# Half of the first x tile through a transposing DMA instead of TensorE

## The chip, the cores and the metric

The kernel runs on one core of a Trainium2 chip. The metric is device time of one execution in microseconds (us), median of several runs. In the profile PE is TensorE's matmuls, PEld its weight loads, DVE VectorE, ACT ScalarE, POOL GpSimd, and SP the engine that here only issues DMAs; `SPq` is its queue of instructions.

## The reference

x is 2048 x 512 in bf16. Two branches read it and a gate per row mixes them.

```python
x = A_x
g = _sigmoid((x * gate_w).sum(-1, keepdims=True))
a = _A_ref(x, A_wq, A_wk, A_wv, A_wo, A_beta)   # attention in 4 segments of 512 rows, 32 heads of 16, with a running memory
b = _B_ref(x, B_W_gate, B_W_up, B_W_down)       # ReLU-gated MLP, 512 -> 1792 -> 512
return g * a + (1 - g) * b
```

Every projection contracts over x's columns, and the kernel feeds each segment to TensorE transposed (`xT`, columns on the partitions); its gate also reads the segment in natural layout (`xn`).

## The kernel before

The kernel is written as a graph of operations. A list scheduler with fixed guessed durations puts them in one order and picks buffers; then the instructions are emitted in that order. Segments 1 to 3 of x come by transposing DMA. Segment 0 is in a hurry: it comes in natural layout, in four quarters over the two DMA queues (SP and ACT), TensorE transposes it in 16 blocks into PSUM (`G`), and DVE and ACT copy the result to `xT`. The q projection of segment 0 runs step by step over the four blocks of 128 columns, so it can begin with half of x.

```python
for i in range(2):                    # halves of x's columns
    for eng, q, h in (("SP", nc.sync, 0), ("ACT", nc.scalar, 1)):
        ...  q.dma_start(out=xn[0].t[:, 2*h:2*h+2, 256*i:256*i+256], in_=x[...])
    if i == 0:   ...                  # wq block 0: one half of its columns on SP, one on ACT
    else:        ...                  # wq block 1 on SP, blocks 2 and 3 on ACT
...                                   # cut: then wk, wv, gate_w and the MLP weights on SP
def first_x(c, after):                # block c of 128 columns
    for h in range(2):
        ...  nc.tensor.transpose(gv[:, t*P:(t+1)*P], xn[0].t[:, 2*h+t, c*P:(c+1)*P], ident[:])
        ...  # DVE copies h == 0 to xT, ACT copies h == 1
first_x(0, None); first_x(1, None)
for ci in range(NC):                  # the four q steps, 4 matmuls each
    ...  nc.tensor.matmul(qS.t[:, c, :], lhsT=wq_sb[:, ci, ...], rhs=xT[0].t[:, ci, :], ...)
    if ci < 2:
        first_x(ci + 2, o_q0)
...                                   # cut: k projection, v projection, attention units, MLP
order = sc.run()
for o in order:
    tiling[0] = o.ran                 # "C": a dense matmul next to column-tiled work
    o.emit(o.eng)                     #      is emitted as four column tiles
```

Emitted as column tiles, a dense matmul takes 4 weight loads and 4 matmuls instead of one each.

Of the kernel before, what the change touches and what calls it, by code (L numbers as in the profile page):

```python
# [9 lines left out]
ACT = mybir.ActivationFunctionType  # L10
ALU = mybir.AluOpType

P = 128
# [5 lines left out]
L = S // NSEG  # L19
F = 1792  # L20
NC = D // P
# [33 lines left out]
class Sched:  # L55
# [5 lines left out]
    def op(self, name, engs, emit, deps=(), key=0.0, cls=1, mode=None, alloc=(), uses=(), land=0.0, flex=False):  # L61
        o = Op()
        o.flex, o.ran = flex, mode
        o.name, o.engs, o.emit, o.key, o.cls, o.mode = name, engs, emit, key, cls, mode
        o.alloc, o.uses = list(alloc), list(alloc) + list(uses)
        o.deps = [d if isinstance(d, tuple) else (d, None) for d in deps]
        o.deps = [d for d in o.deps if d[0] is not None]
        o.start = o.end = o.eng = None
        o.land = land
        o.succ, o.seq = [], len(self.ops)  # L70
        for b in o.uses:
            b.left += 1
        self.ops.append(o)
        return o
# [92 lines left out]
def kernel(  # L167
# [15 lines left out]
    nc = tc.nc  # L183
    x = A_x.flatten_outer_dims()
# [5 lines left out]
    def tl(name, shape, dt=BF16):  # L190
        return sb.tile(list(shape), dt, name=name)
# [9 lines left out]
    wq_sb, wk_sb, wv_sb, wo_sb = (tl(n, [P, NC, D]) for n in ("wq_sb", "wk_sb", "wv_sb", "wo_sb"))  # L201
# [98 lines left out]
    def load(name, emit, nbytes, key, alloc=(), uses=(), deps=(), eng="SP"):  # L300
        o = op(name, {eng: 0.5}, emit, deps=[(d, None) for d in deps] + ([(last_dma[0], -1e9)] if eng == "SP" else []),
               key=key, cls=0, alloc=alloc, uses=uses, land=nbytes / GBs)
        if eng == "SP":
            last_dma[0] = o
        return o

    xn = [Buf(xnp) for _ in range(NSEG)]
    xT = [Buf(xTp) for _ in range(NSEG)]

    def wview(ap):  # L310
        return ap.rearrange("(c p) n -> p c n", p=P)

    lx0, lw, lwq = {}, {}, {}
    for i in range(2):
        for eng, q, h in (("SP", nc.sync, 0), ("ACT", nc.scalar, 1)):
            def f(e, i=i, q=q, h=h):
                q.dma_start(out=xn[0].t[:, 2 * h:2 * h + 2, 256 * i:256 * i + 256],  # L317
                            in_=x[256 * h:256 * h + 256, 256 * i:256 * i + 256].rearrange("(t p) d -> p t d", p=P))
            lx0[i, h] = load(f"x0_{i}{h}", f, 131072, -300 + i, eng=eng, alloc=[xn[0]] if (i, h) == (0, 0) else [],
                             uses=[] if (i, h) == (0, 0) else [xn[0]])  # L320
        if i == 0:
            for eng, q, h in (("SP", nc.sync, 0), ("ACT", nc.scalar, 1)):
                def f(e, h=h, q=q):
                    cs = slice(256 * h, 256 * h + 256)
                    q.dma_start(out=wq_sb[:, 0, cs], in_=A_wq[0:P, cs])  # L325
                lwq.setdefault(0, []).append(load(f"wq0{h}", f, 65536, -299.5, eng=eng))
        else:
            for c0, c1, eng, q in ((1, 2, "SP", nc.sync), (2, 4, "ACT", nc.scalar)):
                def f(e, c0=c0, c1=c1, q=q):
                    q.dma_start(out=wq_sb[:, c0:c1, :], in_=A_wq[c0 * P:c1 * P, :].rearrange("(c p) n -> p c n", p=P))  # L330
                o = load(f"wq{c0}", f, 131072 * (c1 - c0), -298, eng=eng)
                for ci in range(c0, c1):
                    lwq[ci] = [o]

    def loadw(name, tile_, ap, c0, c1, key, eng="SP"):
        def f(e):
            q = nc.sync if eng == "SP" else nc.scalar
            q.dma_start(out=tile_[:, :, c0:c1], in_=wview(ap)[:, :, c0:c1])
        return load(name, f, P * tile_.shape[1] * (c1 - c0) * 2, key, eng=eng)

    lw["wk"] = loadw("wk", wk_sb, A_wk, 0, D, 1)
    lw["wv"] = loadw("wv", wv_sb, A_wv, 0, D, 1)

    def f(e):
        nc.sync.dma_start(out=gwrep[:], in_=gate_w.partition_broadcast(P))
# [36 lines left out]
    xc0 = {c: [] for c in range(NC)}  # L382
    def first_x(c, after):
        for h in range(2):
            g = Buf(G)

            def f(e, c=c, g=g, h=h):
                gv = g.t[:].bitcast(BF16)
                for t in range(2):
                    nc.tensor.transpose(gv[:, t * P:(t + 1) * P], xn[0].t[:, 2 * h + t, c * P:(c + 1) * P], ident[:])  # L390
            a = op(f"xtr{c}{h}", {"PE": 0.2}, f, deps=[lx0[c // 2, h], o_ident, (after, 0.0)], key=-500 + c, mode="D",
                   alloc=[g], uses=[xn[0]])

            def f(e, c=c, g=g, h=h):
                gv = g.t[:].bitcast(BF16)[:, 0:256]
                dst = xT[0].t[:, c, 256 * h:256 * h + 256]
                if e == "DVE":
                    nc.vector.tensor_copy(dst, gv)
                else:
                    nc.scalar.activation(dst, gv, ACT.Copy)  # L400
            xc0[c].append(op(f"xcp{c}{h}", {"DVE": 0.27} if h == 0 else {"ACT": 0.4}, f, deps=[a], key=-500 + c, cls=0,
                             alloc=[xT[0]] if (c, h) == (0, 0) else [], uses=[g] + ([] if (c, h) == (0, 0) else [xT[0]])))
    qS = Buf(Spool)
    q0 = [Buf(QTp) for _ in range(NC)]
    o_q0 = None
    first_x(0, None)
    first_x(1, None)
    for ci in range(NC):
        def f(e, ci=ci):
            for c in range(NC):  # L410
                nc.tensor.matmul(qS.t[:, c, :], lhsT=wq_sb[:, ci, c * P:(c + 1) * P], rhs=xT[0].t[:, ci, :],  # L411
                                 start=(ci == 0), stop=(ci == NC - 1))
        o_q0 = op(f"q0.{ci}", {"PE": 4 * MM * (1.5 if ci < 2 else 1)}, f,
                  deps=xc0[ci] + lwq[ci] + [(o_q0, 0.0) if ci else None],
                  key=-400 + ci, mode="D", alloc=[qS] + q0 if ci == 0 else [], uses=([] if ci == 0 else [qS]) + [xT[0]])
        if ci < 2:
            first_x(ci + 2, o_q0)
    xc0 = [o for c in range(NC) for o in xc0[c]]
    xr = {0: xc0}
    for s in range(1, NSEG):  # L420
        if s > 1:
# [606 lines left out]
```

## Time and profile before

| | before |
|---|---|
| time, median of 3 (lowest, highest) | 267.25 us (266.84, 267.45) |
| profiled span | 265.7 us |
| PE busy | 256.3 us, 96% |
| first matmul of the k projection | 9.78 us |
| start of the last matmul | 262.15 us |

The last two rows are read from PE's timeline; the last matmul is the fourth of the second line:

```profile
9.78 0.59 PE L249 MATMUL G<-xT,wk_sb 128*128 128x512 bf16 x2
261.82 0.60 PE L249 MATMUL G<-wo_sb,oT 128*128 128x256 bf16 x4
```

The execution that was profiled took 267.44 us, at the slow end of the kernel's runs. Before 9.78 us is the *opening*, in which PE waits for loads; after it comes the *later part*, 252.37 us from the first k matmul to the last matmul, in which PE has work nearly all the time.

### The profile page before, as it was taken

What the parts mean: (1) busy time and instruction counts of PE and PEld (TensorE: products, weight loads), DVE (VectorE), ACT (ScalarE), POOL (GpSimd) and SP (SyncE); (2) the same over time, 40 slices, a digit from 0 to 9 for tenths busy, and PEclk for the clock granted to TensorE, in tenths of its full rate; (3) what the DMA queues carried; (4) which work ended last, traced back from release to release, by engine and by line L of the source; (5) the groups of instructions that cost most, each with busy time, mean ns of one, the idle gap of its engine ahead of it and who ended that gap; (6) DMA issues with size and microseconds to landing.
All of it is one profiled execution on the core that took longest, in us unless ns stands there. A gap on an engine that the chain in (4) does not pass through costs nothing.

```text
span 265.7 us, 7041 instructions
## 1 busy us (share of the span) xinstructions
PE 256.3 (96%) x2795; PEld 114.5 (43%) x2832; DVE 182.5 (69%) x404; ACT 195.3 (73%) x191; POOL 188.4 (71%) x467
## 2 busy tenths in 40 slices
PE   7999999999999999999999999999999999999995
PEld 6434444444444444444444434344443444444444
DVE  1397888888975185998888837688985725466611
ACT  3498999899886658899896667898788566777010
POOL 8268888888559688798648988887878866537000
PEclk9999999999999999999999999999999999999999
DMA  6995991016310000000660010000000010000011
GB/s 171 309 268 145 333 241 25 2 38 78 103 23 23 22 20 22 0 2 0 131 109 3 23 42 21 2 0 2 0 2 4 0 42 20 23 2 0 2 41 39
DMA packets 27585, 15.54 MB, mean 58 GB/s; under 512 B 13600, under 2 KB 27552, under 8 KB 27552
## 3 DMA queue, kind: packets, MB, share of 16 engines
q1 hardware_dynamic: 26592, 14.50, 23.2%
q10 hardware_dynamic: 960, 0.59, 0.7%
q8 instruction: 22, 0.36, 0.6%
q14 instruction: 11, 0.09, 0.1%
HBM read 9.84 MB, written 2.10 MB: 45 GB/s over the span
## 4 chain that ended last, share of the span: by engine, by line
PE 95%; issue 2%; DMA 2%; SPq 0%; DVE 0%; DVEq 0%
PE G L249 74%; PE S L740 9%; PE G L852 7%; PE G L247 2%; DMA wq_sb<-in_A_wq_dram 2%; PE S L411 1%; PE G L613 1%; PE G L787 0%; SPq L317 0%; DVE os L702 0%; SPq L325 0%; PE G L390 0%; DVEq L702 0%
## 5 line engine op out<-in xcount | busy, mean ns | idle before, releaser
L754 ACT ACTIVATE E<-S 128x2048 bf16<-128x2048 f32 x72 | 135.1, 1876 | 32.1 <-PE S L740 29.4
L762 POOL TENSOR_SCALAR_AFFINE_SELECT E<-E 64x256 bf16<-64x256 bf16 x256 | 116.2, 454 | 39.2 <-ACT E L754 25.4
L249 PE MATMUL G<-xT,wu_sb 128*128 128x512 bf16 x210 | 57.1, 380 | 0.4 <-issue 0.2
L249 PE MATMUL G<-xT,wg_sb 128*128 128x512 bf16 x207 | 56.3, 380 | 1.1 <-issue 0.8
L665 DVE TENSOR_TENSOR hT<-G,rg 128x512 bf16<-128x512 f32 x56 | 38.2, 683 | 20.0 <-ACT rg L661 10.9
L249 PE MATMUL G<-wd_sb,hT 128*128 128x512 bf16 (+1 forms) x215 | 49.7, 366 | 1.3 <-issue 1.1
L887 DVE STREAM_TRANSPOSE T<-G 128x512 f32<-128x512 f32 x44 | 30.3, 702 | 13.0 <-PE G L852 8.2
L661 ACT ACTIVATE rg<-G 128x512 bf16<-128x512 f32 x56 | 32.7, 597 | 5.6 <-PE G L249 5.3
L249 PEld LDWEIGHTS <-wu_sb 128*128 128x128 bf16 x218 | 19.9, 98 | 24.8 <-issue 3.0
L249 PEld LDWEIGHTS <-hT 128*128 128x128 bf16 x226 | 20.5, 98 | 22.7 <-issue 3.0
L249 PEld LDWEIGHTS <-wg_sb 128*128 128x128 bf16 x218 | 19.4, 98 | 24.6 <-issue 4.1
L740 PE MATMUL S<-QT,K 32*128 32x192 bf16 (+7 forms) x512 | 28.6, 287 | 0.5
L740 PEld LDWEIGHTS <-K 32*128 32x128 bf16 x512 | 8.3, 92 | 30.2 <-issue 29.7
L702 DVE TENSOR_SCALAR os<-G,ngcol 128x512 bf16<-128x512 f32 (+1 forms) x8 | 5.5, 683 | 21.1 <-PE G L249 21.0
L852 PE MATMUL G<-E,Vp 64*32 64x128 bf16 (+7 forms) x512 | 19.0, 284 | 0.4 <-issue 0.4
L852 PE MATMUL G<-E,VS 64*32 64x128 bf16 (+7 forms) x512 | 18.4, 284 | 0.0
L599 POOL COPY VS<-Vp 64x256 bf16<-64x256 bf16 x32 | 12.9, 404 | 7.5 <-DVE Vp L517 6.0
L704 ACT ACTIVATE os<-G,ngcol 128x512 bf16<-128x512 f32 x9 | 6.2, 687 | 15.9 <-PE G L249 15.8
L249 PE MATMUL G<-wo_sb,oT 128*128 128x512 bf16 (+1 forms) x66 | 17.0, 367 | 0.3 <-issue 0.3
L907 DVE TENSOR_TENSOR O<-T,sm 128x256 bf16<-128x256 f32 x32 | 16.0, 529 | 0.3
L249 PE MATMUL G<-xT,wk_sb 128*128 128x512 bf16 x60 | 15.8, 380 | 0.3 <-issue 0.2
L481 POOL COPY R<-rcol 32x4 f32<-32x4 f32 x64 | 13.6, 212 | 3.0
(96 smaller groups left out, 295.5 us busy)
## 6 DMA issues: line engine op xcount, KB each, us to landing
out_dram<-os SPq DMA_DIRECT2D x15, 128.0 KB, 1.7
wd_sb<-in_B_W_down_dram SPq DMA_DIRECT2D x1, 1792.0 KB, 13.9
xn<-in_A_x_dram SPq DMA_DIRECT2D x3, 512.0 KB, 4.9
wg_sb<-in_B_W_gate_dram SPq DMA_DIRECT2D x2, 512.0 KB, 5.3
wu_sb<-in_B_W_up_dram SPq DMA_DIRECT2D x2, 512.0 KB, 6.6
wg_sb<-in_B_W_gate_dram SPq DMA_DIRECT2D x3, 256.0 KB, 6.7
wu_sb<-in_B_W_up_dram SPq DMA_DIRECT2D x3, 256.0 KB, 6.4
wk_sb<-in_A_wk_dram SPq DMA_DIRECT2D x1, 512.0 KB, 5.9
```

What stands on the lines that cost most here:

```text
L249: nc.tensor.matmul(out_ap, lhsT=lhsT, rhs=rhs, start=start, stop=stop)
L481: nc.gpsimd.tensor_copy(R[s][32 * j:32 * j + 32, k, :], rcol[32 * k:32 * k + 32, cols])
L599: nc.gpsimd.tensor_copy(VS[s].t[64 * r:64 * r + 64, t, 0:H // 2 * HP].rearrange("p (h v) -> p h v", v=HP)[:, :, 0:DH], src[:, :, r, 0:DH])
L661: nc.scalar.activation(rg.t[:], g.t[:], ACT.Relu)
L665: nc.vector.tensor_tensor(h.t[:], u.t[:], rg.t[:], ALU.mult)
L704: nc.scalar.activation(ob.t[:, cs], g.t[:, 0:W], ACT.Copy, scale=ngcol[:, tt:tt + 1])
L740: nc.tensor.matmul(sp.t[:, j, off:off + w], lhsT=K2[s, cc].t[rows, kb, :, :].rearrange("p r k -> p (r k)"), rhs=QT[s, cc].t[rows, L - w:L] ...
L754: nc.scalar.activation(eb_.t[:], sp.t[:], ACT.Exp, scale=SCALE)
L762: nc.gpsimd.affine_select(out=v, in_=v, compare_op=ALU.is_ge, fill=0.0, base=0, pattern=[[0, 4], [1, 64]], channel_multiplier=-1)
L852: nc.tensor.matmul(gs[r].t[32 * j:32 * j + 32, L - w:L], lhsT=v, rhs=src.t[rows, j, off:off + w], start=(kb == 0), stop=(kb == 7), tile_po ...
L887: nc.vector.transpose(T.t[:].rearrange("p b e -> p (b e)"), g.t[:])
L907: nc.vector.tensor_tensor(O.t[:, :, r, :], T.t[:, :, 0:DH], sm.t[:, r, :, None].to_broadcast([P, 16, DH]), ALU.mult)
```

## The change

The intent: take half of the transposes and copies off the engines in the opening. The second half of x's columns goes by transposing DMA straight to `xT`; its natural copy, which only the gate needs, comes after wv. The loads of wq are redistributed.

```diff
-    for i in range(2):
-        ... x halves on SP and ACT; wq block 0 split over both; block 1 on SP; blocks 2, 3 on ACT
+    x0_part(0, 0, "SP", -300)
+    x0_part(0, 1, "ACT", -300)
+    wq_rows(0, 1, "ACT", -299)
+    def f(e):
+        nc.sync.dma_start_transpose(out=xT[0].t[:, 2:4, :], in_=x[0:L, 256:512])
+    lxt0 = load("xT0", f, 2 * 262144, -299, alloc=[xT[0]])
+    wq_rows(1, 2, "ACT", -298)
+    wq_rows(2, 4, "SP", -298)
     ... wk, wv
+    for h in range(2):
+        x0_part(1, h, "SP", 1)
 ... (cut)
     first_x(1, None)
+    xc0[2] = xc0[3] = [lxt0]
     for ci in range(NC):
         ...
-        if ci < 2:
-            first_x(ci + 2, o_q0)
```

Because the graph changes, the list scheduler also puts the *rest* of the program in another order. The diff doesn't show that.

More of the change, by code (lines that the diff above doesn't have):

```diff
@@ L313 @@
     lx0, lw, lwq = {}, {}, {}
-    for i in range(2):
-        for eng, q, h in (("SP", nc.sync, 0), ("ACT", nc.scalar, 1)):
-            def f(e, i=i, q=q, h=h):
-                q.dma_start(out=xn[0].t[:, 2 * h:2 * h + 2, 256 * i:256 * i + 256],
-                            in_=x[256 * h:256 * h + 256, 256 * i:256 * i + 256].rearrange("(t p) d -> p t d", p=P))
-            lx0[i, h] = load(f"x0_{i}{h}", f, 131072, -300 + i, eng=eng, alloc=[xn[0]] if (i, h) == (0, 0) else [],
-                             uses=[] if (i, h) == (0, 0) else [xn[0]])
-        if i == 0:
-            for eng, q, h in (("SP", nc.sync, 0), ("ACT", nc.scalar, 1)):
-                def f(e, h=h, q=q):
-                    cs = slice(256 * h, 256 * h + 256)
-                    q.dma_start(out=wq_sb[:, 0, cs], in_=A_wq[0:P, cs])
-                lwq.setdefault(0, []).append(load(f"wq0{h}", f, 65536, -299.5, eng=eng))
-        else:
-            for c0, c1, eng, q in ((1, 2, "SP", nc.sync), (2, 4, "ACT", nc.scalar)):
-                def f(e, c0=c0, c1=c1, q=q):
-                    q.dma_start(out=wq_sb[:, c0:c1, :], in_=A_wq[c0 * P:c1 * P, :].rearrange("(c p) n -> p c n", p=P))
-                o = load(f"wq{c0}", f, 131072 * (c1 - c0), -298, eng=eng)
-                for ci in range(c0, c1):
-                    lwq[ci] = [o]
@@ new lines, in x0_part, with wq_rows, f @@
+    def x0_part(i, h, eng, key):
+        def f(e):
+            (nc.sync if eng == "SP" else nc.scalar).dma_start(
+                out=xn[0].t[:, 2 * h:2 * h + 2, 256 * i:256 * i + 256],
+                in_=x[256 * h:256 * h + 256, 256 * i:256 * i + 256].rearrange("(t p) d -> p t d", p=P))
+        first = not lx0
+        lx0[i, h] = load(f"x0_{i}{h}", f, 131072, key, eng=eng, alloc=[xn[0]] if first else [], uses=[] if first else [xn[0]])
+    def wq_rows(c0, c1, eng, key):
+        def f(e):
+            (nc.sync if eng == "SP" else nc.scalar).dma_start(
+                out=wq_sb[:, c0:c1, :], in_=A_wq[c0 * P:c1 * P, :].rearrange("(c p) n -> p c n", p=P))
+        o = load(f"wq{c0}", f, 131072 * (c1 - c0), key, eng=eng)
+        for ci in range(c0, c1):
+            lwq[ci] = [o]
@@ L335, in loadw, with f @@
+    x0_part(0, 0, "SP", -300)
+    x0_part(0, 1, "ACT", -300)
+    wq_rows(0, 1, "ACT", -299)
+    def f(e):
+        nc.sync.dma_start_transpose(out=xT[0].t[:, 2:4, :], in_=x[0:L, 256:512])
+    lxt0 = load("xT0", f, 2 * 262144, -299, alloc=[xT[0]])
+    lxt0.engs["SP"] = 1.2
+    wq_rows(1, 2, "ACT", -298)
+    wq_rows(2, 4, "SP", -298)
     def loadw(name, tile_, ap, c0, c1, key, eng="SP"):
@@ L401, in first_x @@
             xc0[c].append(op(f"xcp{c}{h}", {"DVE": 0.27} if h == 0 else {"ACT": 0.4}, f, deps=[a], key=-500 + c, cls=0,
-                             alloc=[xT[0]] if (c, h) == (0, 0) else [], uses=[g] + ([] if (c, h) == (0, 0) else [xT[0]])))
+                             uses=[g, xT[0]]))
     qS = Buf(Spool)
@@ L415 @@
                   key=-400 + ci, mode="D", alloc=[qS] + q0 if ci == 0 else [], uses=([] if ci == 0 else [qS]) + [xT[0]])
-        if ci < 2:
-            first_x(ci + 2, o_q0)
-    xc0 = [o for c in range(NC) for o in xc0[c]]
+    xc0 = xc0[0] + xc0[1] + [lxt0]
     xr = {0: xc0}
```

## The prediction

> **What bounds the kernel now.** I read the busy shares first, then the chain that ended last, then that chain in order of time over the first 15 us, then PE's own timeline there, and last the sync engine's timeline, because the change touches only the opening.
>
> ```profile
> span 265.7 us, 7041 instructions
> PE 256.3 (96%) x2795; PEld 114.5 (43%) x2832; DVE 182.5 (69%) x404; ACT 195.3 (73%) x191; POOL 188.4 (71%) x467
> PE 95%; issue 2%; DMA 2%; SPq 0%; DVE 0%; DVEq 0%
> ```
> PE is busy 96% of the span and makes up 95% of the chain; no other engine passes 73%. The stretches (width, then busy time by engine, granted clock, DMA share, GB/s) tell where PE's idle 9.4 us are:
>
> ```profile
> 0.00:4.00 4.00, 2.89 (x28) 2.90 (x29) 0.47 (x11) 1.15 (x1) 3.33 (x8) 1.00 0.44 108
> 4.00:10.00 6.00, 5.18 (x36) 2.63 (x36) 1.10 (x4) 1.78 (x7) 4.60 (x8) 1.00 0.95 290
> 10.00:262.00 252.00, 247.76 (x2734) 108.89 (x2769) 180.50 (x388) 192.36 (x185) 180.52 (x452) 1.00 0.23 53
> 262.00:265.70 3.70, 0.42 (x4) 0.13 (x2) 0.48 (x1) 0.00 (x0) 0.00 (x0) 1.00 0.09 25
> ```
> From 10 us to 262 us PE is 98.3% busy at full clock. So a microsecond saved before 10 us moves the whole rest forward one for one, and nothing that eases DVE, ACT or POOL can pay. The opening is different: there the chain in order of time holds a DMA.
>
> ```profile
> 2.27 4.63 DMA wq_sb<-in_A_wq_dram
> 6.96 1.04 PE S L411 x4
> 7.99 0.22 PE G L390 x4
> 8.22 0.22 PE S L411
> 8.43 0.05 issue
> 8.48 1.46 PE S L411 x6
> 9.94 3.88 PE G L249 x18
> ```
> The load of the second row block of wq, issued at 2.27, ends PE's wait at 6.90. L411 is the first q projection, four steps of four matmuls; L390 is a TensorE transpose of x. The k projection (L249) follows. PE's timeline (start, length) between:
>
> ```profile
> 4.07 0.62 PE L390 MATMUL G<-ident,xn 128*128 128x128 bf16 x8
> 4.93 1.02 PE L411 MATMUL S<-xT,wq_sb 128*128 128x512 bf16 x4 [0.25 <-DVE xT L398]
> 6.34 0.48 PE L390 MATMUL G<-ident,xn 128*128 128x128 bf16 x4 [0.39 <-DMA xn<-in_A_x_dram]
> 6.96 1.04 PE L411 MATMUL S<-xT,wq_sb 128*128 128x512 bf16 x4
> ```
> The second half of x (columns 256 to 511) holds PE until 6.34, just before wq does. Both arrive late because the queues issue four loads each, about 0.5 us apart, and the first byte moves only at about 2.2 us.
>
> [...] the later 512 KB transposes of x land in 4.1 to 5.7 us (one in traffic 9.0), a plain 512 KB load of x in 4.9; but the rate seen while one runs is nearer 200 to 290 GB/s. [...] with both queues filled, 4 to 10 us moved 290 GB/s, and from 10 to 16 us, with SP alone, about as much or a little more. [...] Here one shows 219 ns, and eight took 0.62 us from first start to last end, so they overlap and cost about 0.1 us each. [...] The trace shows a small price: a row-tiled score group between dense groups starts 0.96 us after the dense group's start instead of 0.87 (22.38 to 23.34), and the next dense group 0.33 us later (23.67).
>
> **The change part by part.**
>
> Removed from PE: 8 of 16 transposes. Four took 0.22 us on the chain; the other four stood in 6.34 to 6.96, in the shadow of the wq load that came at 6.90. So 0.2 us is certain, up to 0.8 if data no longer waits. Also gone: two DVE copies (0.29 each) and two ACT copies (0.38 each)[...]; with PE as the bound they count only through PE's wait for the second half.
>
> Moved: x's second half becomes one SP transposing DMA in second place; wq's block 0 goes whole to ACT (second place), block 1 to ACT (third), blocks 2 and 3 to SP, behind the transpose. SP and ACT then issue eight loads without a wait, and these include wk and wv; before, wk waited on a landing and was issued at 3.78.
>
> When does each thing land? The issue times and landing times are from these rows and from the page of DMAs:
>
> ```profile
> 1.31 0.44 SPq L325 DMA_DIRECT2D wq_sb<-in_A_wq_dram  x1
> 3.78 0.38 SPq L338 DMA_DIRECT2D wk_sb<-in_A_wk_dram  x1
> 12.30 5.41 SPq L360 DMA_TRANSPOSE xT<-in_A_x_dram  x1
> ```
> - First half of x: as before, PE transposes at 4.07; first q step at 4.93 (wq block 0, 128 KB issued near 1.3, should land by 4.6: it took 2.9 us for 64 KB, and 64 KB more is 0.2 us at 290 GB/s, plus sharing with the transpose).
> - wq block 1: issued near 1.8 instead of 2.27; at 3.4 to 4.6 us in flight it lands between 5.2 and 6.4. Second q step from about 5.9, end 6.8 (four matmuls, 0.22 us apart, are 0.87).
> - Transposed half: issued near 1.3. A quiet 512 KB transpose holds SP for 1.3 to 2.0 us, one of 128 KB for 1.2, the one behind a full queue 5.41. I take 1.3 us for 256 KB here, when the queue is still short. Landing: 4 us after issue, near 5.5; not needed before 6.8.
> - wq blocks 2 and 3: issued near 2.7, and the same load took 5.0 us before: 7.3 to 7.7. Steps three and four then run 7.4 to about 9.2.
> - wk: issued near 3.2, took 5.9: near 9.1, as the steps end. Before, the k projection began at 9.78.
> Sum: the k projection begins near 9.2 instead of 9.78 to 9.94, a gain of 0.6 to 0.7 us. A check by bytes: x, wq and wk are 1.5 MB in both kernels, some 5.4 us at 290 GB/s; from 2.2 that allows 7.6[...]. So bytes don't forbid 9.2[...].
>
> Added: natural x columns 256 to 511 are still loaded (256 KB), after wv. That is extra traffic of 256 KB, 0.9 us at 290 GB/s, ahead of the gate weights. Those were issued at 6.51 and took up to 6.7, 13.2, while the first gate matmul ran at 16.33: 3 us of slack, hidden. The gating sums that read this copy run at 18.7 us and later, hidden too.
>
> Changed order: the list scheduler reorders the rest of the program. I counted the built programs: the same matmuls but for the eight transposes (and four dense ones no longer split into column tiles), and 172 changes of tiling mode against 170. A score group costs 0.33 + 0.09 = 0.42 us over the dense rhythm, of which 0.22 is its own stream of 512 columns: about 0.1 us per change, so 0.2 us lost.
>
> Net: 0.65 gained, 0.2 given back, about 0.45 us: 267.25 - 0.45 = **266.8 us**.
>
> **The rivals.**
> A, **the transpose blocks the queue**: if it holds SP 2.7 us (half of 5.41), wq blocks 2 and 3 are issued near 4.0, land near 9, and q ends near 10.8, wk behind it near 10.5. That costs 0.9 us: 268.3. For it: the 5.41 us row. Against: that one followed 1 MB of queued weights; quiet ones took 1.3 and 2.0.
> B, **hidden anyway**: wk's arrival binds, as the trace's 0.24 us wait of the weight load on wk before 9.69 suggests, and the bytes come no sooner. Then the k projection starts near 9.7 and the time stays at 267.2 to 267.4.
> C, **the order decides**: some later stage meets a score group or a value product that isn't ready. The kernel before idles 4.24 us between 10 and 262; a fifth more or less of that is 0.8 us either way.
> D, **everything early**: if all loads come by 7.3, the k projection starts at 8.6, gain 1.3 minus 0.2: 266.1.
>
> **Range and chances.** D and a lucky order give about 265.6, A with a little of C 268.3. The runs of before spread from 266.84 to 267.45. So 265.6 to 268.3 for 8 in 10. Two per cent are 5.3 us, more than half of PE's whole idle time: faster 0.01. Slower by 5.3 would need a stall that nothing in the trace shows: 0.02. Same: 0.97.
>
> **What would show it.** Right: L390's counterpart has 8 matmuls; the first k matmul starts between 8.6 and 9.5; wk issued near 3.2; the transpose is busy on SP for about 1.3 us; PE's idle from 10 us on stays within 1 us of 4.24. Wrong: SP stuck in the transpose past 3.5 us or the first q step later than 5.2 (rival A), a wait of PE for wk with a start near 9.7 (B), or an equal gain at 10 us that has vanished by the end (C). A total over 269 would mean that a wait for gate weights or for the score chain arose that I put down as hidden.

Beside two figures belongs what the trace of before shows. The flight of 3.4 to 4.6 us for wq block 1 was the estimate: that block took 4.6 us, and the four x loads of the same 128 KB took 2.7 to 4.7. The "first byte at about 2.2 us": from 1.8 to 2.1 us 38 GB/s moved, from 2.1 to 2.4 us 114, from 2.4 to 2.7 us 273.

## More of the kernel before

All runs quoted here were fast, with a granted TensorE clock of 0.998 to 1.000.

PE's own instructions come through a DMA queue too, and one line of the page that I passed over at first becomes important:

```profile
q8 instruction: 22, 0.36, 0.6%
```

That is 22 transfers of 16 KB over the execution (number, MB, share of 16 engines). That the queue is PE's is read from counts: no other engine has more than 531 instructions in these traces, and in the three kernels below that have 156 to 180 PE instructions fewer, it carries 21 transfers.

## The result and the profile after

| | before | changed |
|---|---|---|
| time, median of 4 (lowest, highest) | 267.16 us (266.84, 267.45) | 267.63 us (267.31, 267.82) |
| ratio, 95% interval | | 1.0017 (0.9999 to 1.0034) |
| profiled span | 265.7 us | 265.9 us |
| first k matmul | 9.78 us | 9.59 us |
| later part (first k matmul to last matmul) | 252.37 us | 252.78 us |

A ratio here is the mean time of one kernel's fast runs over that of the other's from the same rounds, so it isn't quite the ratio of the medians. Two more measurements of the same two kernels gave 1.0020 (0.9999 to 1.0041) and 1.0034 (1.0018 to 1.0051): slower by some 0.2 to 0.3%, 0.5 to 0.9 us in the medians.

The page and the stretches of the changed kernel (stretch, width, busy time of PE, PEld, DVE, ACT, POOL, clock, DMA share, GB/s) first:

```profile
span 265.9 us, 7000 instructions
PE 256.3 (96%) x2776; PEld 114.2 (43%) x2812; DVE 184.3 (69%) x404; ACT 192.8 (73%) x187; POOL 188.3 (71%) x467
```
```profile
4.00:10.00 6.00, 4.68 (x27) 2.04 (x26) 0.52 (x2) 0.87 (x3) 4.61 (x8) 1.00 1.11 283
10.00:262.00 252.00, 248.08 (x2720) 108.89 (x2754) 182.87 (x390) 190.49 (x183) 180.37 (x452) 1.00 0.21 53
```

The shares are those of before. From 4 to 10 us PE did 0.5 us less work, as it should with 8 transposes fewer, in the same six microseconds: the relief was mostly turned into waiting. The busy time from 10 to 262 us is even higher than before, although that part turns out longer; matmul ends are modelled and some records are missing, so this figure can't resolve half a microsecond. The page of before has 2,795 matmuls for 2,832 weight loads, that of the changed kernel 2,776 for 2,812. Run 2 below has a matmul for every weight load, and PE's idle time there is 0.85 us, not 4:

```profile
10.00:262.00 252.00, 251.15 (x2768) 108.38 (x2766) 180.69 (x389) 191.78 (x184) 180.22 (x452) 1.00 0.21 53
```

So most of the idle time on the two pages is missing records. Marks such as the first k matmul and the last matmul are safe; the changed kernel's last matmul, 262.37, is the fourth of this line:

```profile
262.05 0.60 PE L249 MATMUL G<-wo_sb,oT 128*128 128x256 bf16 x4
```

The chain of work in the opening (start, length, what):

```profile
2.71 5.10 DMA wq_sb<-in_A_wq_dram
7.81 0.05 issue
7.85 1.25 PE S L420 x5
9.11 0.05 issue
9.16 0.59 PE S L420 x2
9.75 3.88 PE G L249 x18
```

It is the chain of before with other numbers: a load of wq, now blocks 2 and 3 behind the transpose, holds the q steps (L420 here) until 7.81 us. PE's and SP's timelines in the opening:

```profile
3.92 0.61 PE L398 MATMUL G<-ident,xn 128*128 128x128 bf16 x8
4.77 1.02 PE L420 MATMUL S<-xT,wq_sb 128*128 128x512 bf16 x4 [0.25 <-DVE xT L406]
6.64 1.04 PE L420 MATMUL S<-xT,wq_sb 128*128 128x512 bf16 x4 [0.84 <-DMA wq_sb<-in_A_wq_dram]
7.85 1.90 PE L420 MATMUL S<-xT,wq_sb 128*128 128x512 bf16 x7 [0.18 <-DMA wq_sb<-in_A_wq_dram]
9.59 2.75 PE L249 MATMUL G<-xT,wk_sb 128*128 128x512 bf16 x12
```
```profile
1.31 1.34 SPq L335 DMA_TRANSPOSE xT<-in_A_x_dram  x1
2.71 0.56 SPq L324 DMA_DIRECT2D wq_sb<-in_A_wq_dram  x1
3.31 0.47 SPq L344 DMA_DIRECT2D wk_sb<-in_A_wk_dram  x1
```

The eight transposes are gone as planned and SP is held for only 1.34 us. But the second q step begins at 6.64 instead of 6.96, no more than 0.3 us earlier: wq block 1, issued at 1.85 us, landed at 6.59. Here are the landings that matter, in us (from the records of the DMAs):

| | wq block 1 | second half of x | wq blocks 2, 3 | wk |
|---|---|---|---|---|
| before | 6.91 | 6.30 and 6.50 | 7.38 | 9.65 |
| changed | 6.59 | 6.83 | 7.81 | 9.31 |

So the opening gains 0.19 us in these two profiles, and the later part loses 0.41 us. The question for the experiments: is either figure real, and where does the later part lose it? Two stalls of PE stand out in the trace of the changed kernel. The first, near 134 us, waits for DVE, which has the MLP product (hT) behind another product in its queue:

```profile
133.12 0.57 DVE L554 TENSOR_TENSOR pq<-pq,etq 128x512 bf16<-128x512 bf16 x1
133.61 0.68 DVE L672 TENSOR_TENSOR hT<-G,rg 128x512 bf16<-128x512 f32 x1
134.34 1.02 PE L249 MATMUL G<-xT,wu_sb 128*128 128x512 bf16 x3 [0.26 <-DVE hT L672]
```

The second, near 80 us, has no semaphore behind it. The weight loads of a column-tiled run of dense matmuls pause for 0.26 us:

```profile
79.20 1.19 PEld L247 LDWEIGHTS <-hT 128*32 128x32 bf16 x22
80.64 1.20 PEld L247 LDWEIGHTS <-hT 128*32 128x32 bf16 x26 [0.26 <-issue]
```

"issue" means that the engine waited for nothing that the profile shows.

### The profile page after: what moved, and what is told of

The parts are those of the page before. It is cut to its first block, busy times and chain, and to the rows that moved or that the text cites. A ratio compares the mean times of both kernels' runs of the same rounds, so it can differ in the third digit from the quotient of the medians.

```text
span 265.9 us, 7000 instructions
## 1 busy us (share of the span) xinstructions
PE 256.3 (96%) x2776; PEld 114.2 (43%) x2812; DVE 184.3 (69%) x404; ACT 192.8 (73%) x187; POOL 188.3 (71%) x467
## 4 chain that ended last, share of the span: by engine, by line
PE 93%; DMA 2%; DVE 2%; issue 2%; SPq 1%; DVEq 0%
PE G L249 74%; PE S L747 9%; PE G L859 6%; PE G L247 2%; DMA wq_sb<-in_A_wq_dram 2%; PE S L420 1%; DVE hT L672 1%; DVE pk L554 1%; SPq L335 1%; PE G L620 0%; DVE T L894 0%; PE G L794 0%; DVE os L709 0%; SPq L316 0%; DVE pq L553 0%
## 5 line engine op out<-in xcount | busy, mean ns | idle before, releaser
L769 POOL TENSOR_SCALAR_AFFINE_SELECT E<-E 64x256 bf16<-64x256 bf16 x256 | 114.9, 449 | 38.2 <-ACT E L761 24.1
L249 PE MATMUL G<-xT,wu_sb 128*128 128x512 bf16 x212 | 58.2, 380 | 1.1 <-issue 0.5
L249 PE MATMUL G<-xT,wg_sb 128*128 128x512 bf16 x212 | 57.7, 380 | 0.4 <-issue 0.2
L249 PE MATMUL G<-wd_sb,hT 128*128 128x512 bf16 (+1 forms) x213 | 49.0, 365 | 1.4 <-issue 1.3
L606 POOL COPY VS<-Vp 64x256 bf16<-64x256 bf16 x32 | 14.4, 452 | 7.4 <-DVE Vp L524 5.8
L709 DVE TENSOR_SCALAR os<-G,ngcol 128x512 bf16<-128x512 f32 (+1 forms) x10 | 7.0, 696 | 17.5 <-PE G L249 17.4
L249 PE MATMUL G<-wo_sb,oT 128*128 128x512 bf16 (+1 forms) x64 | 16.4, 366 | 0.1
L711 ACT ACTIVATE os<-G,ngcol 128x512 bf16<-128x512 f32 x7 | 4.8, 687 | 15.9 <-PE G L249 15.9
L859 PEld LDWEIGHTS <-Vp 64*32 64x32 bf16 x512 | 12.2, 91 | 8.1 <-issue 3.8
```

What stands on the lines that cost most here:

```text
L249: nc.tensor.matmul(out_ap, lhsT=lhsT, rhs=rhs, start=start, stop=stop)
L606: nc.gpsimd.tensor_copy(VS[s].t[64 * r:64 * r + 64, t, 0:H // 2 * HP].rearrange("p (h v) -> p h v", v=HP)[:, :, 0:DH], src[:, :, r, 0:DH])
L709: nc.vector.tensor_scalar(ob.t[:, cs], g.t[:, 0:W], ngcol[:, tt:tt + 1], None, ALU.mult)
L769: nc.gpsimd.affine_select(out=v, in_=v, compare_op=ALU.is_ge, fill=0.0, base=0, pattern=[[0, 4], [1, 64]], channel_multiplier=-1)
L859: nc.tensor.matmul(gs[r].t[32 * j:32 * j + 32, L - w:L], lhsT=v, rhs=src.t[rows, j, off:off + w], start=(kb == 0), stop=(kb == 7), tile_po ...
```

## The experiments

**Theory O:** the opening gains a little, and the new order of the rest loses more. **Rival P:** the opening itself does harm later. **Rival N:** all of it is scatter. Since the order comes from the scheduler alone, opening and order can be exchanged: keep one kernel's graph (hence its order) and let the operations of the opening emit the other kernel's instructions. Comparing the built programs engine by engine confirmed that only instructions of the opening, and the waits on its loads, differ; the traces agree for runs 2 and 3.

### 1. The changed kernel once more

No edit; it runs on the same chip as the next three.

> The changed kernel once more, so that the next three are compared on one chip. From its first profile: PE's first weight load of the k projection starts at 9.38 us (9.69 in the kernel before), the last weight load of PE comes 0.22 us later than before. Expected: 0.1 to 0.6 us slower than the kernel before (ratio 1.000 to 1.002), and the two PE stalls that its first trace shows and the trace of before does not (0.3 us near 134.0 us, 0.26 us near 80.6 us) are there again.

Measured: 267.81 us against 267.08 of before, ratio 1.0020 (0.9999 to 1.0041). Both stalls were there; the one near 80 us had grown. In its trace:

```profile
79.16 1.19 PEld L247 LDWEIGHTS <-hT 128*32 128x32 bf16 x22
81.33 1.19 PEld L247 LDWEIGHTS <-hT 128*32 128x32 bf16 x26 [0.98 <-issue]
```

The same 22 weight loads, then a pause of 0.98 instead of 0.26 us: its place is fixed by the program, its length isn't.

### 2. New opening, old order

```diff
 # kernel before, its graph untouched; the DMA operations emit other transfers:
-x0_00: x half 0, SP   wq00: wq block 0a, SP   x0_10: x half 1, SP     wq1: wq block 1, SP
-x0_01: x half 0, ACT  wq01: wq block 0b, ACT  x0_11: x half 1, ACT    wq2: wq blocks 2, 3, ACT
+x0_00: x half 0, SP   wq00: transpose, SP     x0_10: wq blocks 2, 3, SP   wq1: nothing
+x0_01: x half 0, ACT  wq01: wq block 0, ACT   x0_11: wq block 1, ACT      wq2: nothing
+wv:    wv, then the natural copy of x's second half, SP
-xtr2*, xtr3*, xcp2*, xcp3*: TensorE transposes and copies
+xtr2*, xtr3*, xcp2*, xcp3*: nothing
```

> The opening of the changed kernel (transposing DMA, its load order, 8 TensorE transposes), but every engine's instruction order after the opening is that of the kernel before. Theory O (the opening gains 0.2 to 0.3 us, and the scheduler's new order loses 0.4 to 0.5 us later): k projection at 9.38 us as in the changed kernel, and the whole 0.2 to 0.3 us faster than before, so 0.4 to 0.7 us faster than the changed kernel. Rival P (the opening itself costs later: the transposing DMA delays the later loads and their users): as slow as the changed kernel, 0.1 to 0.5 us slower than before. Rival N (differences under 0.5 us are noise of the run): all equal to before within 0.1 us.

Measured: 266.36 us against 267.08, ratio 0.9976 (0.9956 to 0.9996): faster than both kernels, correct, and the only member of this group that is. Rival P falls. The size exceeds the expectation; the first k matmul came at 8.86 us in its profile, with the very same instructions that brought it at 9.59 and 9.55 in the two profiles of the changed kernel.

### 3. Old opening, new order

```diff
 # changed kernel, its graph untouched; the reverse exchange:
-xT0: transpose, SP
+xT0: nothing
-wq0: wq block 0, ACT      wq1: wq block 1, ACT       wq2: wq blocks 2, 3, SP
+wq0: wq block 0a SP, 0b ACT
+wq1: x half 1 on SP and ACT, wq block 1 SP, wq blocks 2, 3 ACT      wq2: nothing
-x0_10, x0_11: natural copy of x's second half
+x0_10, x0_11: nothing
+q0.0, q0.1: followed by the TensorE transposes and copies of blocks 2 and 3
```

> The converse: the opening of the kernel before (16 TensorE transposes, its load order), and every engine's order after the opening from the changed kernel. Theory O: k projection at 9.7 us, the later stalls near 80 and 134 us are there, 0.4 to 0.7 us slower than before, the slowest of the four. Rival P: equal to before within 0.15 us. Rival N: all equal.

Measured: 267.70 us, ratio 1.0023 (1.0007 to 1.0038), 0.62 us slower than before, as theory O says. The stall at 134 us is there. But this kernel was *not* the slowest of the four: with the new order the new opening gains nothing (267.81 against 267.70). And the pause near 80 us is gone:

```profile
78.98 2.49 PEld L247 LDWEIGHTS <-hT 128*32 128x32 bf16 x48
```

All 48 weight loads run through. I had not foreseen that the opening would decide over this pause.

### 4. A plain load in place of the transposing DMA

```diff
-nc.sync.dma_start_transpose(out=xT[0].t[:, 2:4, :], in_=x[0:L, 256:512])
+nc.sync.dma_start(out=xT[0].t[:, 2:4, :], in_=x[0:256, :].rearrange("(c p) n -> p c n", p=P))
```

This fills `xT` with untransposed data; the result is wrong (relative error 0.53).

> The changed kernel with the transposing DMA replaced by a plain DMA of the same 256 KB into the same tile (1 KB rows). Results are wrong on purpose. Theory X (the transposing DMA moves 256 B packets slower and holds up the wq loads beside it): the wq block 1 lands near 5.5 us instead of 6.6, blocks 2 and 3 before 7.3 instead of 7.8, wk near 8.8 instead of 9.3; k projection at 8.9 to 9.1 us, and the whole about 0.3 to 0.5 us faster than the changed kernel. Rival Q (issue order and the sum of bytes decide, not the kind of DMA): the loads land within 0.2 us of the changed kernel, and the time is the same.

Measured: 267.88 us, ratio 1.0029 (1.0012 to 1.0047), the same as the changed kernel: the gain that theory X promised isn't there. The plain load itself landed 3.56 us after its issue, the transpose 4.9 to 5.6 us (seven profiles). The other landings fit neither expectation. wq block 1 came at 6.93 us, later than beside the transpose (5.97 to 6.72 in the seven). Blocks 2 and 3 came at 7.19 and wk at 8.68, as X said, but inside the scatter of the seven (6.75 to 7.81, 8.24 to 9.41).

The run doesn't separate the kind of DMA from the order of issue. The plain load held SP for 0.46 us instead of 1.34, so wq blocks 2 and 3 went out at 1.81 us instead of 2.70 and moved beside block 1. The packet records suggest that the kind does matter to a neighbour: of the 128 packets of wq block 1 (1 KB each), 44 to 74 took over 100 ns beside the transpose (seven profiles), 8 beside the plain load; the usual time is 46 ns. A transpose moves smaller packets: in the kernel before, from 61 to 65 us, 1,053 of them held 0.27 MB, some 256 bytes each. With little beside it, a 512 KB transpose moved 280 GB/s there (130.5 to 132 us), a plain 512 KB load of x 356 (66.5 to 68 us). In run 4, though, a plain load gains no time here, and what held wq block 1 stays open.

### 5. Fewer PE instructions in the column-tiled runs

By now the pause near 80 us had a suspect. In the traces of runs 1, 2 and 4 and in the first one of the changed kernel, a pause without a semaphore ended 1.39 to 1.50 us after a 16 KB transfer of the instruction queue had ended. How many instructions such a transfer, a *block* from here on, holds can be estimated from counts. PE of the kernel before has 2 x 2,832 = 5,664 weight loads and matmuls for 22 transfers, some 257 each; between the starts of the first and the last transfer (19.00 and 250.85 us) it began 2,652 weight loads, so about 5,304 instructions for 21 transfers, some 253 each. Around 78 us a value product (64 weight loads, 64 matmuls in 1.1 us), a memory update (another 64 and 64 in 0.7 us) and the column-tiled run stand next to each other, and the next transfer ends 3.5 us after this one (79.26 and 82.74 in the first trace); elsewhere they are mostly 10 to 15 us apart.

Test: emit the dense matmuls in these runs whole, same order.

```diff
-            tiling[0] = o.ran
+            tiling[0] = "D"
```

> The changed kernel with the same order of operations, but the 26 dense matmuls that follow column-tiled work are emitted whole (one weight load and one matmul each) instead of as four column tiles: 156 PE instructions fewer. Theory I (PE waits there for its own instructions: in four traces a PE stall without a semaphore, 0.14 to 0.86 us long near 80 us, ends 1.39 to 1.50 us after the end of a 16 KB transfer of the instruction queue, wherever that falls): the stall near 80 us is gone, and the kernel gains 0.2 to 0.9 us less about 0.1 us for each of 3 or 4 more changes of tiling mode: 0 to 0.6 us faster than the changed kernel. Rival W (the stall is a wait for data, such as hT or wd): it stays, and the time rises by the mode changes, 0.1 to 0.4 us.

Measured: 267.29 us, ratio 1.0010 (0.9997 to 1.0023). The pause is gone; the run of 12 dense matmuls is whole:

```profile
79.19 2.36 PEld L249 LDWEIGHTS <-hT 128*128 128x128 bf16 x12
```

That is the outcome of theory I; with data to wait for, the pause would have stayed. The median is 0.18 us over before, where the changed kernel was 0.47 to 0.90 over; this comparison is across chips, each with its own runs of before, and the intervals of the ratios overlap, so a gain in time isn't shown.

### 6 and 7. The same edit in two kernels with the old order

> New opening with the old order (the fastest so far, 0.7 us faster than before), with the dense matmuls emitted whole. Theory I: its stall near 77.6 to 78.25 us (0.43 us, 1.46 us after an instruction transfer ended) is gone; 0 to 0.4 us faster than with the split. Rival W: not faster.

> The kernel before with the dense matmuls emitted whole, as a control. Theory I: the 0.53 us stall in the value products near 46 us (ended 1.49 us after an instruction transfer) is gone or shorter, since 24 dense matmul records just before it become 6; 0.0 to 0.4 us faster than before. Rival W: 0.1 to 0.4 us slower than before by the mode changes.

Measured: 267.08 us (ratio 0.9999, 0.9986 to 1.0012) and 267.13 us (1.0007, 0.9993 to 1.0021). The pause of the kernel before was this one, in the value products near 46 us:

```profile
45.86 0.20 PE L852 MATMUL G<-E,Vp 64*32 64x64 bf16 x3
46.41 0.19 PE L852 MATMUL G<-E,Vp 64*32 64x64 bf16 x1 [0.35 <-issue]
```

In both new traces the pauses are gone, but neither kernel gains, and run 6 missed its expectation: it lost the advantage of run 2. The trace shows a price: from the first weight load of the memory updates and the small denominators to the next other load, 2.70 us pass in all instead of 2.05, where the tiling mode now changes after them. The later part is 252.20 us in both runs; the old order with split matmuls has 251.83 where it has no pause (runs 10 and 12) and 252.37 in the profile of before. So whole matmuls cost about as much as the pauses that they remove.

### 8. wq ahead of the transpose

```diff
 # run 2, order of issue on SP
-x half 0, transpose, wq blocks 2 and 3, wk
+x half 0, wq blocks 2 and 3, transpose, wk
```

> New opening with the old order, but on SP the load of wq blocks 2 and 3 goes ahead of the transposing DMA. Theory X (the transposing DMA's 256 B packets hold up the 1 KB packets of wq beside them): wq block 1 and blocks 2 and 3 land by 6.0 us, the transposed half lands last, near 6.5; k projection between 8.6 and 9.2 us, equal to e1's or up to 0.4 us earlier. Rival B (the k projection is bound by wk's landing, which no order of the earlier loads moves): k starts within 0.3 us of e1's and the time is that of e1 within 0.2 us.

Measured: 266.53 us, ratio 0.9977 (0.9963 to 0.9992), run 2's advantage within 0.2 us. But the opening went otherwise than either theory said: wq block 0 landed at 6.18 us, where it had come by 4.6 before, so the first q step waited, and the first k matmul came at 9.69. Why is open: in run 4, too, 256 KB of plain load stood second on SP, and there wq block 0 came at 4.68.

### 9 to 11. Opening and order once more

One profile of an opening proves little: with identical instructions wk landed anywhere from 8.24 to 9.41 us. So the cells were measured again.

> The four cells of opening by order once more on one chip (the kernel before is the fourth cell), since single openings scatter: wk landed at 9.31, 9.41, 8.62, 8.24 and 8.76 us in five profiles of the new opening, at 9.65, 9.25 and 9.07 us in three of the old. If opening and order add up (opening about -0.2 us, order about +0.5 us, from the traces), this is 0.2 to 0.5 us slower than before.

> New opening, old order again. Additive theory: 0.1 to 0.4 us faster than before; first k matmul to last matmul 252.0 to 252.4 us, as in all five profiles of the old order so far (251.97 to 252.37). If the first result (0.7 us faster) was the true size: 0.5 us or more faster again.

> Old opening, new order again. Additive theory: 0.4 to 0.7 us slower than before; first k matmul to last matmul at least 252.6 us, as in all five profiles of the new order so far (252.62 to 253.49). If the order costs nothing and the first result was chance: equal to before within 0.2 us.

Medians in us; before was 267.08 on the first chip and 267.03 on the second:

| | old order | new order |
|---|---|---|
| old opening | 0 (before) | +0.62, +0.78 |
| new opening | -0.72, -0.50 | +0.73, +0.90 (changed kernel) |

Ratios of the second set: 1.0034 (1.0018 to 1.0051) for the changed kernel, 0.9980 (0.9968 to 0.9993) for the new opening with the old order, 1.0033 (1.0019 to 1.0047) for the reverse. Rival N falls: the new order costs about 0.7 us by itself, twice. The later part, from first k matmul to last matmul, says the same without overlap: 251.83 to 252.37 us in seven profiles of the old order (mean 252.07), 252.55 to 253.49 in seven of the new (mean 252.92).

My "additive theory" falls too. The new opening is worth 0.5 to 0.7 us with the old order, and costs 0.1 us with the new one. The pause near 80 us can account for most of that. In the new order it looks like this (all times in us):

| opening | transfer of the block ended | column-tiled run began | extra time in the run |
|---|---|---|---|
| old (run 3) | 78.40 | 78.98 | none |
| old (run 11) | 78.71 | 79.28 | none |
| new (first trace) | 79.26 | 79.20 | 0.15 |
| new (run 9) | 79.36 | 78.85 | 0.46 |
| new (run 4) | 79.62 | 79.19 | 0.59 |
| new (run 1) | 79.83 | 79.16 | 0.88 |

The extra time is the time from the first weight load of the run to the next other load, less the 2.92 us that this takes in the two cells without a pause. In the two traces in which the block arrived 0.57 and 0.58 us ahead there is none; in the other four, the later it came, the longer the pause (run 9 and run 4 are out of line by 0.1), and the weight loads went on 1.25 to 1.50 us after the transfer had ended. Without 8 transposes the PE program has 16 instructions less ahead of this place, so block boundaries, if they lie at fixed counts of instructions, move by 16 against the work. The records of the weight loads, which are complete, fit this. With the new opening the run breaks after 22 of its 48 loads; with the old one it has a kink of 0.15 us after 14, some 1.38 us after the transfer ended. Counted from the start of the program, both are the same place, after PE's 862nd weight load. In run 2, with the old order, a pause of 0.26 us also follows the 862nd. The pause of the kernel before near 46 us stands at its 478th load, 384 loads and as many matmuls earlier: 768 instructions, or 769 by the matmul records: for three blocks that is 256 each, between the two estimates of run 5 (253 and 257). So the pauses fit places where blocks meet, and the opening decides which work stands there. What sets how late a block arrives isn't shown, and no run moved the boundary alone; one that pads the program by 16 instructions would.

This also changes how the cells are read. Without a pause the later part took 251.83 us in the old order (runs 10 and 12, alike to 0.01 us) and 252.55 in the new (run 11), so the order itself costs some 0.7 us. The kernel before had 0.53 us of pause near 46 us in its one profile, and runs 2, 8, 10 and 12 have none there. So part of what the new opening gains with the old order is probably a missing pause, and not an earlier k projection.

### 12. Loads in the order of use

```diff
 # run 2, order of issue
-SP: x half 0, transpose, wq blocks 2 and 3, wk     ACT: x half 0, wq block 0, wq block 1
+SP: x half 0, wq block 1, transpose, wk            ACT: x half 0, wq block 0, wq blocks 2 and 3
```

> Old order; opening with the transposing DMA, but wq block 1 second on SP, the transpose third, and wq blocks 2 and 3 third on ACT, so that loads come in the order of use. If the second q step's wait for wq block 1 (landing 6.0 to 6.7 us in the new opening) is what holds the k projection: block 1 lands by 5.2, the first weight load of k comes at 8.6 to 9.0 us (mean 9.16 before) and the kernel is 0.3 to 0.6 us faster than the kernel before. If the sum of bytes decides: first q step later, as with wq blocks 2 and 3 ahead (6.2 us there), and k at 9.1 or later.

Measured: 266.37 us against 267.03, ratio 0.9984 (0.9968 to 0.9999), correct. wq block 1 landed at 3.98 us and the q steps run without a wait; PE's timeline:

```profile
5.17 3.61 PE L436 MATMUL S<-xT,wq_sb 128*128 128x512 bf16 x15
8.62 1.67 PE L249 MATMUL G<-xT,wk_sb 128*128 128x512 bf16 x7
```

The second q step's wait for wq block 1 was indeed what held this opening. The profiled execution, at 265.71 us, was the fastest of its six, so the profile flatters it; the median is 0.7 us below before, hardly different from run 10 on the same chip (266.53). Runs 2, 8, 10 and 12 all beat the kernel before, by some 0.2%; which of their three openings is best these runs don't tell.

## Why the prediction was right or wrong

The time, 267.63 us, lies in the predicted range, which was wide enough for the loss, and within 2% of before. The forecast of a gain of 0.45 us was wrong in sign: it became a loss of 0.47 to 0.90. By its steps:

- **PE is the bound and the opening moves the end one for one.** Right as far as tested: run 12 began the k projection 0.75 us before run 10, with the same later part, and its span is 0.74 us shorter. The 98.3% of the prediction understated it, for most of the 4.24 us of idle were missing records.
- **Transposes and copies removed, SP held 1.3 us, wk issued near 3.2.** Right: 8 matmuls at L398, 1.34 us, 3.31 us. Rival A (a blocked queue) is out.
- **wq block 1 between 5.2 and 6.4 us, the transposed half near 5.5.** Too early: 6.59 and 6.83 (5.97 to 6.72 and 6.21 to 6.96 over all seven profiles). The second step began at 6.6 instead of 5.9. I had allowed block 1 a flight of 3.4 to 4.6 us; it took 4.1 to 4.9. The bytes issued before it are 640 KB in both kernels, so they don't explain it.
- **k near 9.2, gain 0.6 to 0.7.** The first profile shows 9.59, gain 0.19, outside the 8.6 to 9.5 named as the sign of being right. Over all profiles the first weight load of k comes at 9.18 us on average with the new opening (seven) and at 9.51 with the old (four), a gain of 0.34, half of what was forecast; the 0.5 to 0.7 us timed with the old order probably contain a missing pause. A single profile couldn't have judged it, as the scatter of 0.8 us shows. Rival B is a part of it: in two of the seven profiles k waited for wk itself.
- **Gate weights hidden.** Right: issued at 7.41, landed at 13.10; the first gate matmul ran at 16.14.
- **"172 changes of tiling mode against 170 ... so 0.2 us lost."** This is the step that failed. I priced the new order by counting mode changes; it costs 0.62 to 0.78 us with the old opening. The count itself was right: the traces of runs 2 and 3 have 170 and 172 changes. What it left out are waits: about 0.3 us for DVE's hT near 134 us, which all seven traces of the new order have, and about 0.1 us near 125 us. The remaining 0.3 us of the 0.7 between later parts without a pause is found by difference only and isn't placed. With the new opening the instruction pause comes on top, 0.15 to 0.88 us. My rival C named the cause and got too little weight. That its size fits ("0.8 us either way") is luck: it was a fifth of 4.24 us of idle time, most of which was missing records.
- **What would show it.** "PE's idle from 10 us on stays within 1 us of 4.24" held (3.92) and showed nothing: the later part became 0.41 us longer all the same. And I had not thought of the instruction queue.

So the expected gain did not vanish in the opening. It was there, about half as large as forecast, and the reordered rest took it back: by some 0.7 us of the order's own, of which a wait for DVE is the largest piece found, and by a pause of 0.15 to 0.88 us that fits a wait for PE's own instructions.

## What to carry to other kernels

When a scheduler emits the program, an edit at one end reorders the other; exchange opening and order between the two kernels before you judge the edit, and keep the order that is better. On an engine that has work nearly all the time, look for pauses without a semaphore and set them against the transfers of the instruction queue: here a run behind 128 weight loads and 128 matmuls, which took 1.1 and 0.7 us, paused for 0.15 to 0.88 us and went on 1.25 to 1.50 us after such a transfer had ended. Compare the number of matmuls with that of weight loads before you read an idle time. Judge gains under 1 us by several timed rounds and by marks in the trace, not by busy sums or one profile.
